# Moving key transposes under the first inversion and starting the second one a chunk early, with a slope that holds for any alpha

## The chip, the cores and the metric

The kernel runs on one core of one Trainium2 chip. The time is that of the device in microseconds from launch to end, the median of several runs. TensorE does the matrix products, VectorE and ScalarE take their results out of PSUM and do elementwise work, POOL (GpSimd) helps with elementwise work on SBUF, SP issues nearly all DMAs.

## What is computed

A delta-rule attention over 4 x 8 heads, 768 steps of 48 dimensions, and behind it a two-layer network with a parametric ReLU on the 3072 x 384 result:

```
k_n = k / (norm(k) + 1e-6)
for t in range(S):
    y[:, :, t] = q[t] @ state
    state += beta[t] * outer(k_n[t], v[t] - k_n[t] @ state)
x = y as (B*S, H*D)
h = x @ w_in                       # 384 -> 2048
g = max(h, 0) + alpha * min(h, 0)  # alpha per column, 0 to 0.3
out = g @ w_out                    # 2048 -> 384
```

## The kernel before, in words

The sequence is cut into 12 chunks of 64. A step is one chunk for two of the four batches, so there are 24 steps, n = 0 to 23, and two steps make a chunk of 256 tokens for the network. Within a chunk the recurrence becomes a triangular system, whose 32 x 32 blocks are inverted on VectorE for four steps at once (NJ = 4): inversion m serves steps 4m to 4m + 3.

All five queues are ordered by hand: instructions run on each engine in the order in which the program issues them. `weave` interleaves several generators in proportion to the parts that each has.

What a step needs before its recurrence:

- `load_early(n)` loads its keys into one of three buffers (SP). `squares(n)` squares them on ScalarE (L347) and adds up on VectorE (L349). `weigh(n)` takes the root (ScalarE, L357 and L358), a reciprocal (VectorE, L364) and two small products on POOL (L366, L367).
- `flips(n, q)` transposes the keys of step n and the queries of step q on TensorE (L377, four each); ScalarE copies them out (L398, L400).
- `grams(n)` multiplies keys with keys on TensorE (L424); VectorE weighs the result into `same` and `right` (L430, twice); `keep` copies parts with POOL or ScalarE (L473, L477).

An inversion, `eliminate(m)`, has 43 pieces: four transposes on VectorE (L489), a select on POOL (L506), 30 elimination steps of two VectorE instructions (L516, L522), eight transposes (L489). The first inversion is done by `eliminate_small` (L551 to L563) on half blocks, and `cross` puts the halves together (TensorE L593, L603, L610; ScalarE L598; VectorE L617, L619). `place` spreads the results (ScalarE L642, L648, L659; VectorE L638), `between_1` and `between_2` finish them (TensorE L709, L722, and L674 from step 4 on; VectorE L729).

The recurrence of a step is `through_state` (TensorE L763, VectorE L773 and L444), `solve` (L788, L792), `outputs` and `next_state` (L801, L817; VectorE L807, L825), `to_ffn` (transposes L840, copy L842).

The network reads `w_in` and `w_out` after a conversion: DMA into a staging place (L209), two ScalarE instructions (L225, L226, begun by `begin_in`) and two on VectorE (L235, L240, `convert`). `ffn_in(c)` makes 48 products for a chunk (L931), in eight pairs of columns that take turns in two PSUM banks `p_ffn`; behind each pair comes the activation: with `al_t` = alpha - 1, ScalarE makes relu((alpha - 1) h) for each of the two columns (L942) and VectorE adds h (L945). `ffn_out` makes the output products (L972 for chunks 0 and 1, L994 and L1245 later), `ffn_in_fast` serves chunks 8 to 11 with its own slope (L1197, L1202).

The order at the start: keys of steps 0 to 3 (`statics`), queries, then `busy(BUSY)`, which issues eight matrix products of 512 columns (L1389) whose results nobody reads, beside the first inversion on VectorE; `first_chunk` (steps 0 and 1); `second_pair` (steps 2 and 3), woven with `ffn_in(0)`, weight conversion, and the keys, norms and grams of steps 4 to 7; then a weave of `ffn_in(1)` with conversion, steps 8 and 9's keys and the first 15 pieces of the second inversion; then `ffn_out(0)` with the other 28 pieces; then `prelude(4)` with part of `ffn_out(1)`. Three PSUM pairs `p_pair` rotate as `big`.

## Time and profile before

| what | us |
|---|---|
| median of 3 runs | 668.64 (668.08 to 668.86) |
| the profiled execution | 667.61 |
| its span, first to last instruction | 665.9 |
| TensorE busy (share of the span) | 645.7 (97%) |
| VectorE busy | 468.3 (70%) |
| ScalarE busy | 287.9 (43%) |
| POOL busy | 97.8 (15%) |

A line of a timeline gives start, length, engine, line of the kernel, instruction, what it writes and reads, and in brackets how long its engine had been idle and what ended that. PE is TensorE, PEld its weight loads, DVE VectorE, ACT ScalarE. A matrix product of fp32 appears as two records. Records of neighbouring instructions on one engine overlap a little, so a start-to-start distance is shorter than a length.

### The profile page before, as it was taken

The page shows a single profiled execution, that of the slowest core. Times are in us where ns is not written, and L with a number is a line of the kernel's source. Part 1 is how long each engine was busy: PE and PEld are TensorE (multiplying, and loading weights), DVE is VectorE, ACT ScalarE, POOL GpSimd, SP SyncE. Part 2 cuts the span into 40 slices and gives each one's busy share as a digit, 9 for nine tenths or more (in the row PEclk, how much of TensorE's full clock was granted, in tenths as well). Part 3 has the DMA queues.
Part 4 walks back from the last instruction along what each step waited for, and adds up shares of the span by engine and source line. Part 5 has one row for each costly group of instructions (what it writes and reads, how often), then busy time and mean ns, then how long its engine had stood idle before and what let it go on. Part 6 is the DMA issues. An engine that isn't in the chain of part 4 may idle for free.

```text
span 665.9 us, 22115 instructions
## 1 busy us (share of the span) xinstructions
PE 645.7 (97%) x9551; PEld 570.0 (86%) x9551; DVE 468.3 (70%) x1084; ACT 287.9 (43%) x717; POOL 97.8 (15%) x201
## 2 busy tenths in 40 slices
PE   6989899999999999999999999999999999999997
PEld 5577788656688998988998998998999999999997
DVE  4965779868989958747949747858866656557363
ACT  4937767335456344334344334234236246052150
POOL 6000112001010000001000000000035044063260
PEclk9999999989999999999999999999999999999999
DMA  8847754211342032122111112112111210100000
GB/s 128 243 119 197 194 112 120 72 35 27 69 80 49 12 64 49 24 52 48 24 41 36 21 43 38 22 41 37 25 41 35 40 36 2 28 10 1 25 1 25
DMA packets 110962, 37.72 MB, mean 57 GB/s; under 512 B 104160, under 2 KB 107248, under 8 KB 110864
## 3 DMA queue, kind: packets, MB, share of 16 engines
q1 hardware_dynamic: 109088, 35.81, 24.6%
q8 instruction: 75, 1.23, 0.8%
q10 hardware_dynamic: 1776, 0.49, 0.4%
q14 instruction: 23, 0.19, 0.1%
HBM read 31.56 MB, written 4.72 MB: 54 GB/s over the span
## 4 chain that ended last, share of the span: by engine, by line
PE 84%; DVE 10%; ACT 3%; issue 2%; DMA 1%; ACTq 0%; DVEq 0%
PE p_ffn L931 22%; PE p_ffn L994 17%; PE p_more L1245 8%; PE p_more L1162 4%; PE p_ffn L1152 3%; PE p_ffn L1245 3%; PE p_pair L377 3%; PE p_ffn L1157 2%; PE p_pair L763 2%; PE p_pair L424 2%; PE p_pair L788 2%; PE p_pair L674 2%; PE p_pair L801 2%; DVE prod L516 2%; DVE block L522 2%; PE p_pair L1389 2%
## 5 line engine op out<-in xcount | busy, mean ns | idle before, releaser
L931 PE MATMUL p_ffn<-xt,w_in 128*128 128x256 f32 x768 | 175.0, 382 | 1.8 <-DVE act L945 1.0
L931 PEld LDWEIGHTS p_ffn<-xt,w_in 128*128 128x128 f32 x768 | 142.9, 190 | 21.9 <-DVE act L945 1.6
L942 ACT ACTIVATE act<-p_ffn,al_t 128x256 f32<-128x256 f32 x112 | 46.8, 468 | 75.5 <-PE p_ffn L931 75.2
L945 DVE TENSOR_TENSOR act<-act,p_ffn 128x512 f32<-128x512 f32 x56 | 38.2, 682 | 39.2 <-ACT act L942 39.0
L1186 POOL TENSOR_TENSOR k_t<-k_t 128x128 f32<-128x128 f32 (+1 forms) x48 | 32.2, 670 | 164.8 <-ACT k_t L1181 162.2
L522 DVE TENSOR_TENSOR block<-block,prod 128x30 f32<-128x30 f32 (+9 forms) x150 | 49.9, 333 | 5.2
L516 DVE TENSOR_TENSOR prod<-block 128x30 f32<-128x30 f32 (+9 forms) x150 | 48.9, 326 | 1.8
L842 ACT COPY xt<-p_pair 128x384 f32<-128x384 f32 x22 | 10.4, 480 | 91.1 <-PE p_pair L840 77.3
L994 PE MATMUL p_ffn<-w_out,act 128*128 128x192 f32 x288 | 49.7, 329 | 0.0
L366 POOL TENSOR_TENSOR beta_t<-beta_t,rec 128x8 f32<-128x8 f32 x24 | 6.3, 261 | 285.9 <-DVE rec L364 265.7
L994 PEld LDWEIGHTS p_ffn<-w_out,act 128*128 128x128 f32 x288 | 46.5, 190 | 0.6 <-DVE act L945 0.3
L1186 POOL TENSOR_TENSOR block<-block 128x128 f32<-128x128 f32 (+1 forms) x48 | 29.5, 616 | 14.7 <-ACT block L1181 12.1
L1152 PE MATMUL p_ffn<-xt,w_in 128*128 128x256 f32 x96 | 28.7, 380 | 0.0
L686 ACT COPY inv<-p_pair 32x256 f32<-32x256 f32 x40 | 14.4, 361 | 22.4 <-DVE u L792 21.4
L773 DVE TENSOR_TENSOR r<-v_raw,p_pair 64x192 f32<-64x192 f32 (+1 forms) x66 | 23.2, 352 | 1.2
L792 DVE TENSOR_TENSOR u<-p_pair,wgt 128x384 f32<-128x384 f32 x24 | 13.3, 556 | 15.1 <-PE p_pair L674 14.8
L1014 DVE TENSOR_TENSOR o_sb<-u,p_ffn 128x192 f32<-128x192 f32 x24 | 7.9, 351 | 20.2 <-PE p_ffn L994 19.8
L1245 PE MATMUL p_more<-w_out,act 128*128 128x192 f32 x128 | 22.0, 329 | 0.0
L349 DVE TENSOR_REDUCE norm<-ksq 128x8 f32<-128x384 f32 x24 | 13.1, 547 | 12.7 <-ACT ksq L347 12.6
L642 ACT ACTIVATE inv<-inverse,which 128x256 f32<-128x256 f32 x44 | 21.6, 504 | 0.2
L752 ACT COPY y<-p_pair 128x384 f32<-128x384 f32 x22 | 10.4, 478 | 26.0 <-PE p_pair L748 23.9
L1181 ACT COPY k_t<-p_more 128x512 f32<-128x512 f32 x16 | 9.4, 585 | 28.0 <-PE p_more L1162 25.1
(224 smaller groups left out, 1423.1 us busy)
## 6 DMA issues: line engine op xcount, KB each, us to landing
w_out<-in_moe_w_in_dram SPq DMA_DIRECT2D x12, 512.0 KB, 5.1
qp<-in_q_dram SPq DMA_DIRECT2D x48, 96.0 KB, 3.0
v_raw<-in_v_dram SPq DMA_DIRECT2D x48, 96.0 KB, 2.9
kl<-in_k_dram SPq DMA_DIRECT2D x96, 48.0 KB, 2.7
out_dram<-o_sb SPq DMA_DIRECT2D x92, 48.0 KB, 1.6
space_out<-in_moe_w_out_dram SPq DMA_DIRECT2D x11, 384.0 KB, 4.2
ke<-in_k_dram SPq DMA_DIRECT2D x43, 96.0 KB, 3.2
w_out<-in_moe_w_out_dram SPq DMA_DIRECT2D x5, 384.0 KB, 4.0
```

The costliest lines, as they stand in the source:

```text
L516: nc.vector.tensor_tensor(out=prod, in0=r[:, 0:j, j : j + 1].to_broadcast([128, j, n]), in1=r[:, j : j + 1, j + 1 : HB].to_broadcast([128, ...
L522: nc.vector.tensor_tensor(out=r[:, 0:j, j + 1 : HB], in0=r[:, 0:j, j + 1 : HB], in1=prod, op=ALU.add)
L642: nc.scalar.mul(out, x, which[:, i : i + 1])
L773: nc.vector.tensor_tensor(out=r[to, a], in0=v_in[to, a], in1=p[own, a, :, 0:D], op=ALU.subtract)
L931: nc.tensor.matmul(p_h[:, i], w_in[:, t, (f + i) * 128 : (f + i + 1) * 128], xt[:, t], start=(t == 0), stop=(t == KT - 1),)
L942: nc.scalar.activation(g[:, i], p_h[:, i], ACT.Relu, scale=al_t[:, f + i : f + i + 1])
L945: nc.vector.tensor_tensor(out=g, in0=g, in1=p_h, op=ALU.add)
L994: nc.tensor.matmul(p, x(i), w(i), start=(i == 0), stop=(i == FP - 1))
L1152: nc.tensor.matmul(p[:, f * 256 : f * 256 + 256], w(2, f), xt[:, 2], start=True, stop=False)
L1162: nc.tensor.matmul(q[:, j], a, b, start=True, stop=True)
L1186: nc.gpsimd.tensor_tensor(out=dst, in0=a, in1=b, op=ALU.add)
L1245: nc.tensor.matmul(p, x(i), w(i), start=(i == 0), stop=(i == FP - 1))
```

## The change

Three things are changed together.

1. The keys of steps 4, 5 and 6 are squared, transposed, and for 4 and 5 multiplied to grams, right behind the queries, between shorter fillers (`busy(2)` and three times `busy(1.25)` in place of `busy(8)`). One of the three PSUM pairs is set aside meanwhile to hold the two grams. Their norms, weights and gram evictions follow inside `first_chunk`. The fetch of the first six pieces of `w_in` is issued behind these keys' loads, and its conversions begin later: one ahead of the first inversion's end, three more behind the first cross products, two behind `between_2`. `second_pair` keeps only what is left of steps 6 and 7.
2. The second inversion, `eliminate(1)`, starts in `second_pair`: 4, 3, 3 and 3 of its pieces are woven in from the step behind `scale_v` on. Thirteen more, not fifteen, go beside `ffn_in(1)`, and the last 17 beside `ffn_out(0)`.
3. The activation becomes relu(-h) for both columns in one ScalarE instruction, and on VectorE, column by column, relu(-h) times (1 - alpha) plus h; so in `ffn_in` and in `ffn_in_fast`.

```diff
--- before.py
+++ after.py
@@ -307,7 +307,7 @@
     def slopes():
         p = ps_one()[:, 0:FT]
         nc.tensor.transpose(p, al_sb, ident[:FT, :FT])
-        nc.scalar.activation(al_t, p, ACT.Copy, bias=-1.0)
+        nc.scalar.activation(al_t, p, ACT.Copy, scale=-1.0, bias=1.0)
 
 
     beside = [const.tile([128, 2, G, D + C], FP32, name=f"beside{bp}") for bp in range(NB)]
@@ -340,14 +340,20 @@
         squares(n)
         now(weigh(n))
 
+    ksq = {}
+
+    def squared(n):
+        ksq[n] = work.tile([128, H, D], FP32, name="ksq", bufs=2)
+        nc.scalar.square(ksq[n], early(n)[:, :, 0:D])
+
+    def norms(n):
+        stats[n] = work.tile([128, H], FP32, name="norm", bufs=EARLY + 3)
+        nc.vector.tensor_reduce(out=stats[n], in_=ksq.pop(n), axis=AXX, op=ALU.add)
+
     def squares(n):
-        if n >= N:
-            return
-        ksq = work.tile([128, H, D], FP32, name="ksq", bufs=2)
-        nc.scalar.square(ksq, early(n)[:, :, 0:D])
-        norm = work.tile([128, H], FP32, name="norm", bufs=EARLY + 3)
-        nc.vector.tensor_reduce(out=norm, in_=ksq, axis=AXX, op=ALU.add)
-        stats[n] = norm
+        if n < N:
+            squared(n)
+            norms(n)
 
     def weigh(n):
         if n >= N:
@@ -424,9 +430,9 @@
             nc.tensor.matmul(
                 p[half(t), a, g], k_t[n][dims(a), g, half(t)], k_t[n][dims(a), g, half(t)]
             )
-        w = stats[n][1][:, 0:2, :, None].to_broadcast([128, 2, G, HB])
 
         def weighted(dst, cols):
+            w = stats[n][1][:, 0:2, :, None].to_broadcast([128, 2, G, HB])
             nc.vector.tensor_tensor(
                 out=dst.rearrange("p (a g) i -> p a g i", a=2), in0=p[:, :, :, cols], in1=w,
                 op=ALU.mult,
@@ -938,11 +944,12 @@
                         yield
 
             g = act_of(c, f // 2)
+            nc.scalar.activation(g, p_h, ACT.Relu, scale=-1.0)
             for i in range(2):
-                nc.scalar.activation(
-                    g[:, i], p_h[:, i], ACT.Relu, scale=al_t[:, f + i : f + i + 1]
+                nc.vector.scalar_tensor_tensor(
+                    out=g[:, i], in0=g[:, i], scalar=al_t[:, f + i : f + i + 1], in1=p_h[:, i],
+                    op0=ALU.mult, op1=ALU.add,
                 )
-            nc.vector.tensor_tensor(out=g, in0=g, in1=p_h, op=ALU.add)
             gs.append(g)
             if c >= FAST and f == FT // 2 - 2:
                 later = operand_sums(0)
@@ -1193,13 +1200,14 @@
                 )
 
             def below():
+                nc.scalar.activation(r, g, ACT.Relu, scale=-1.0)
+
+            def slope():
                 for f in range(2):
-                    nc.scalar.activation(
-                        r[:, f], g[:, f], ACT.Relu, scale=al_t[:, 2 * i + f : 2 * i + f + 1]
+                    nc.vector.scalar_tensor_tensor(
+                        out=g[:, f], in0=r[:, f], scalar=al_t[:, 2 * i + f : 2 * i + f + 1],
+                        in1=g[:, f], op0=ALU.mult, op1=ALU.add,
                     )
-
-            def slope():
-                nc.vector.tensor_tensor(out=g, in0=r, in1=g, op=ALU.add)
 
             due.put(PER * (i + 1) + {0: PER, FP - 1: 2}.get(i, 3), total)
             due.put(PER * (i + 2) + {FP - 2: 1, FP - 1: -4}.get(i, 2), below)
@@ -1424,22 +1432,30 @@
         next(middle)
         pause.append(ps_one())
         busy(1, pause[0])
-        begin_in(6)
+        begin_in(4)
         for i in both:
             scale_v(i)
             mask(i)
         convert(2)
+        for i in both:
+            norms(NJ + i)
         next(middle)
         busy(1.25)
         place(0, (0,))
+        rest = weigh(NJ) + weigh(NJ + 1)
         place(1, (0,), True)
         for i in both:
             place(i, (1,), True)
             now(between_1(i))
         busy(0.5, ps_ffn())
+        now(rest)
+        now(waiting)
+        big.append(aside)
         for i in both:
             place(i, (2,))
             now(between_2(i))
+        begin_in(6)
+        squared(NJ + 2)
         for i in both:
             now(through_state(i))
             now(solve(i))
@@ -1510,11 +1526,11 @@
         load_v(n)
     load_late(0)
     nc.sync.dma_start(out=al_sb, in_=moe_alpha.rearrange("(f p) -> f p", p=128))
-    fetch_in(n_in)
     squares(0)
     betas()
     for _ in statics(0, NJ - 1):
         pass
+    fetch_in(n_in)
     nc.scalar.copy(inside, ones)
     edges(0, edge)
     load_late(1)
@@ -1530,8 +1546,18 @@
     for i in range(2):
         place(i, (3,))
 
-    busy(BUSY)
-    begin_in(4)
+    aside = big.pop(0)
+    busy(2)
+    for n in range(NJ, NJ + 3):
+        if n < NJ + 2:
+            squared(n)
+        flips(n, N)
+        busy(1.25)
+        if n == NJ + 1:
+            waiting = grams(NJ, aside[:, :, 0 : G * C])
+    waiting += grams(NJ + 1, aside[:, :, 256 : 256 + G * C])
+    load_early(NJ + NKE)
+    begin_in(1)
     for _ in eliminate_small(0):
         pass
     n = 12
@@ -1552,60 +1578,52 @@
 
     def second_pair():
 
-        n = 2
-        both, x = (n, n + 1), NJ
+        n, last = 2, 2 * NJ - 1
+        both = (n, n + 1)
         halves = [cross(0, slice(i * H, i * H + H), edge, half_way) for i in both]
-        squares(x)
+        norms(last - 1)
+        now(weigh(last - 1))
         alongside(4, 2)
         for h in halves:
             next(h)
-        flips(x, n)
-        load_early(x + NKE)
+        flips(last, n)
+        load_early(last + 1)
         load_q(n + 2)
-        squares(x + 1)
+        squares(last)
         alongside(5, 2)
         next(halves[0])
-        flips(x + 1, n + 1)
-        load_early(x + 1 + NKE)
+        flips(N, n + 1)
+        load_early(last + 2)
         load_q(n + 3)
-        now(weigh(x))
+        now(weigh(last))
         place(n, (0,))
         alongside(4, 2)
         next(halves[1])
-        now(weigh(x + 1))
+        now(grams(last - 1))
         place(n + 1, (0,))
         alongside(4, 2)
         for i in both:
             now(between_1(i))
-        now(grams(x))
-        squares(x + 2)
+        now(grams(last))
+        load_early(last + 3)
         alongside(5, 3, (chain(*(placing(i, (1, 2, 3)) for i in both)), 6))
         for i in both:
             now(between_2(i))
-        now(grams(x + 1))
         for i in both:
             scale_v(i)
-        flips(x + 2, N)
-        load_early(x + 2 + NKE)
-        now(weigh(x + 2))
-        alongside(5, 3)
+        alongside(5, 3, (part(blocks, 4), 4))
         y = ps_big()
         pieces = []
         for i in range(2):
             pieces += through_state(n + i, None, y[:, :, i * G * D : (i + 1) * G * D])
         now(pieces)
-        squares(x + 3)
-        alongside(5, 3)
+        alongside(5, 3, (part(blocks, 3), 3))
         y = ps_big()
         pieces = []
         for i in range(2):
             pieces += solve(n + i, y[:, :, i * G * D : (i + 1) * G * D])
         now(pieces)
-        now(grams(x + 2))
-        flips(x + 3, N)
-        load_early(x + 3 + NKE)
-        now(weigh(x + 3))
-        alongside(5, 2)
+        alongside(5, 2, (part(blocks, 3), 3))
         pieces = []
         for i in both:
             y = ps_big()
@@ -1614,15 +1632,14 @@
         for i in both:
             load_late(i + 2)
             load_v(i + 3)
-        alongside(5, 2)
+        alongside(5, 2, (part(blocks, 3), 3))
         for i in both:
             to_ffn(i)
-        now(grams(x + 3))
         alongside(IN_PARTS - 42, 1)
 
+    blocks, SOON, LAST = eliminate(1), 13, 6
     second_pair()
     fetch_out(len(stages))
-    blocks, SOON, LAST = eliminate(1), 15, 6
     weave(
         (part(conv_out, PARTS_OUT - 10 - LAST), PARTS_OUT - 10 - LAST), (ffn_in(1), IN_PARTS - 4),
         (statics(2 * NJ, FIRST + 3), 2 * (FIRST + 4 - 2 * NJ) + 1), (part(blocks, SOON), SOON),
@@ -1633,7 +1650,7 @@
     load_early(FIRST + NJ + NKE)
     load_q(NJ + 2)
     weave(
-        (conv_out, OUT_PARTS // 2), (part(blocks, WHOLE + PIECES - SOON), WHOLE + PIECES - SOON),
+        (conv_out, OUT_PARTS // 2), (part(blocks, WHOLE + PIECES - 13 - SOON), WHOLE + PIECES - 13 - SOON),
         (ffn_out(0, True), OUT_PARTS),
     )
```

## The prediction

> **What bounds the kernel now.** First the page's busy line, then the table of stretches, whose columns are busy time and instruction count of each engine, granted clock, DMA share and GB/s.
>
> ```profile
> PE 645.7 (97%) x9551; PEld 570.0 (86%) x9551; DVE 468.3 (70%) x1084; ACT 287.9 (43%) x717; POOL 97.8 (15%) x201
> ```
> ```profile
> 20.00:30.00 10.00, 10.00 (x108) 4.48 (x102) 9.01 (x31) 9.61 (x20) 0.00 (x0) 1.00 0.96 239
> ...
> 48.70:72.30 23.60, 20.38 (x508) 16.98 (x508) 13.24 (x31) 17.18 (x41) 2.19 (x6) 1.00 0.79 188
> 72.30:95.20 22.90, 22.77 (x521) 19.96 (x522) 18.15 (x42) 14.59 (x37) 4.51 (x10) 1.00 0.62 168
> 95.20:119.30 24.10, 23.92 (x176) 20.33 (x175) 21.63 (x57) 17.60 (x42) 4.71 (x10) 1.00 0.45 113
> 119.30:140.10 20.80, 20.80 (x66) 11.96 (x64) 17.75 (x51) 4.68 (x11) 0.78 (x2) 1.00 0.16 39
> 140.10:150.00 9.90, 8.40 (x143) 5.32 (x142) 4.55 (x11) 5.35 (x14) 0.41 (x2) 0.83 0.26 61
> 150.00:222.00 72.00, 69.43 (x1254) 54.38 (x1247) 65.08 (x156) 36.13 (x97) 6.24 (x14) 1.00 0.27 52
> 222.00:500.00 278.00, 278.00 (x4115) 256.79 (x4114) 201.10 (x478) 105.07 (x275) 12.01 (x27) 1.00 0.19 37
> ```
>
> From 222 us on TensorE never rests, so what happens earlier only shifts the end, microsecond for microsecond. Before that VectorE is nearly as full as TensorE: 18.2 of 22.9 us in the stretch of the second pair of steps, 21.6 of 24.1 in the second chunk's input products, 65.1 of 72 after 150. Between 119 and 140 TensorE (output products of the first chunk) is the longer of the two. Next the timelines of TensorE and VectorE around the edits:
>
> ```profile
> 20.17 9.22 PE L1389 MATMUL p_pair<-k_t,ident 112*128 112x512 f32 x16
> ...
> 119.32 20.81 PE L972 MATMUL p_ffn<-w_out,act 128*128 128x384 f32 x64
> 141.63 0.69 PE L674 MATMUL p_pair<-diag,right 32*32 32x32 f32 x32 [1.50 <-ACT diag L648]
> ```
> ```profile
> 78.40 1.11 DVE L773 TENSOR_TENSOR r<-v_raw,p_pair 128x192 f32<-128x192 f32 x3
> ...
> 91.33 0.69 DVE L945 TENSOR_TENSOR act<-act,p_ffn 128x512 f32<-128x512 f32 x1 [1.35 <-ACT act L942]
> ...
> 95.39 0.69 DVE L945 TENSOR_TENSOR act<-act,p_ffn 128x512 f32<-128x512 f32 x1 [2.25 <-ACT act L942]
> ...
> 139.19 1.94 DVE L489 STREAM_TRANSPOSE turned<-block 128x256 f32<-128x256 f32 x4
> ```
>
> The 9.22 us of L1389 are filler beside the first inversion. At 140 TensorE waits 1.50 us: the second inversion's transposes end on VectorE at 141.1, ScalarE copies, L674 starts. Idle time of VectorE between 72 and 120 that later work could fill is small: 1.35 and 2.25 above, and 0.50, 0.94, 0.44 in the same timeline, 5.5 in all.
>
> [...] the clock reads 0.63, 0.50 and 0.74 in the three 1.5 us slices from 143.5 to 148, right after the wait at 140. [...] the rows L430 and L945 show 415 to 419 and 682. [...] L398 (immediate, 512 wide) takes 583, L942 (pointer, 256) 468, two of them 0.84 us: so one 512-wide instruction in their place saves some 0.25.
>
> **The change, part by part.** Sums are against the profiled execution: span 665.9, own time 667.61, 1.03 below the median of 668.64. I add the sum to the median.
>
> *Filler replaced (20 to 30 us).* Filler falls from 8 units to 2 + 3 x 1.25 = 5.75; three key transposes (L377) and two gram groups (L424) come in. The 16 filler records start 0.85 us apart until 24.5 and 0.43 after, so at this clock: 4 records 3.6, first transpose 0.9, three fillers at 1.08 = 3.2, two transposes at 0.48, two gram groups at 0.55. Sum 9.8 against 9.2: the cross products (L593) start **0.6 later**. Nothing hides that: VectorE's transposes, which L593 needs, are ready at 28.05, and all after it is one chain. Bounds: -0.5 (warm earlier) to +2 (a transpose waits for a copy behind ScalarE's zeros, which end at 23.7).
>
> *Queues.* SP issues steps 4 to 6's keys (six DMAs, 3.9 us at 0.65 each) ahead of the six w_in pieces. w_in then lands near 22 to 29; its first conversion is now at about 29 and four more follow the first cross product, so ScalarE does not wait. The loads behind (late keys, v, q) are not read before 46. Step 7's key DMAs come after its buffer is free at 24.5. Cost 0. If DMA is still full, cost up to 1. On ScalarE squares, copies and weighing (some 4 us) fit its idle 1.2 before 38.1 and 4.0 before 44.2 once conversions are spread. On VectorE two norms (1.0) fit before L617 (idle 1.15), and two reciprocals and four gram evictions (1.7) fit the idle 3.19 before L729; POOL's eight small operations and four copies run while it is idle from 19 to 60. Cost 0; uncovered, up to 1.
>
> *48.7 to 72.3.* Here the same transposes and grams remain as before (step 6's and 7's grams move up where 4's stood). ScalarE loses a square (0.43) and that 0.25 per slope, ahead of the 0.89 wait of L722 for it: **-0.6**. TensorE's waits on "issue" (0.27, 0.59, 1.21) move to other places with the changed instruction stream: -1 to +1, taken as -0.4. With the first part: -0.4 at 72.
>
> *72 to 120.* TensorE loses three transposes and grams here, 2.8 us. VectorE is what counts. Removed: three gram evictions (0.73 each), a norm 0.46, two reciprocals 0.24: 2.9. Added: 26 pieces of the second inversion instead of 15, the difference being elimination steps 11 to 21, which the timeline has from 122.5 to 133.3 with 1.95 of conversions between: 8.9. The slope, thirteen pairs of columns from here: one 512-wide L945 (0.60 start to start) becomes two 256-wide instructions with a per-partition scalar. No row shows that form. Below, two plain ones: 2 x 0.34, +0.08. Above: L638, 256 wide with such a scalar at double rate, takes 0.349 where L235's 0.42 for 512 at the same rate implies 0.29, so the scalar costs 0.06, twice: +0.20. A gain is excluded, since two fixed costs replace one. I take **+0.18**, 2.3 in all. Net 2.9 out, 11.2 in: +8.3. Of the idle 5.5 the 0.94 hangs on a ScalarE queue that waits for w_out DMAs, themselves released by VectorE's conversions; 4.5 to 5 can be filled. So the last slope of the second chunk ends **3.4 later**. Order of the waits: four turns ahead of r delay L773 and so L788; elimination steps ahead of u delay L801; those ahead of y delay L840; then L945 holds one of two p_ffn banks and L931 waits. L972's second product needs the last L945, hence with -0.4, **+3.0** at 120.
>
> *120 to 150.* VectorE now has 9 steps (5.6), 8 transposes (4.1) and 3 of other work beside 20.8 of TensorE: done by 138. L648 still stands behind two o_sb copies, the second ending at 140.64, so only **0.55** of the 1.50 goes; the copies are late next. [...] half rate for 3.4 us cost **1.7**, which I count as saved. +0.75 here.
>
> *After.* 150 to 222: eight slopes at 0.18 on a VectorE with 65.1 of 72 us, half of it reaching TensorE: **+0.7**. After 222: VectorE at 72% absorbs it, ScalarE is 0.25 shorter per pair: 0, bounds -0.5 to +1.5.
>
> Sum: -0.4 + 3.4 - 0.55 - 1.7 + 0.7 = +1.45, with rounding upward for the unfilled waits **+1.6**: 670.2, slower by just over the 0.2% (1.3 us) that a measurement of this kernel can tell from no change.
>
> **Rivals.** *Wash.* The scalar costs nothing (+0.08 per pair: 1.0 and 0.3 in place of 2.3 and 0.7): -0.1, giving 668.5. For it: L945's PSUM operand costs nothing extra either. Against: L638. *Faster: VectorE fits.* Place: the second chunk's slopes. If also the "issue" wait before 67.5 vanishes (-1.2) and all idle is filled (-1.0), the debt at 120 falls to +0.4 with the cheap slope, the wait and throttle give back 2.2: 666.5. It decides where the last L945-like slope ends before 120.5. For it: TensorE does lose 2.8 us of work there. Against: VectorE was already full from 73.7 to 90. *Worse.* The throttle still falls (+1.7), or falls in the new waits of 80 to 97; 672 to 673.6.
>
> **Numbers.** Full VectorE, clock kept or not: 0.50 (own range 668.8 to 673.6). Wash 0.25, faster 0.25. Range 666.0 to 673.6: it leaves out the faster case's far end and a throttle with a late start. Chances: faster 0.26, same 0.26, slower 0.48.
>
> **What would show it.** Right: VectorE without idle from 74 to 122; the two new slope instructions 0.47 to 0.49 each; new TensorE waits before L788, L801 and L931 between 80 and 97 on VectorE; L972 of the first chunk starting near 122; the wait before L674 near 1.0; clock 1.00 around 145. Wrong: L972 starting at or before 119.3, or VectorE idle over 3 us between 74 and 122.

## The result, and the profile after

The changed kernel takes 675.89 us (median of 4 runs, 674.84 to 676.93) against 668.47 for the kernel before: a ratio of 1.0116, interval 1.0081 to 1.0151. It is slower, as forecast to be likeliest, but by 7.4 us, not 1.6, and above the range. Here and below, medians are over all runs of a kernel, while ratios and their intervals leave out the few runs that lie more than 1.5% above the fastest of the same kernel, which makes a ratio a little kinder to a kernel that scatters much. The profiled execution took 674.84 us, its span 673.1 (before: 667.61 and 665.9).

The page of the kernel after, its busy line and the clock in 40 slices of the span:

```profile
PE 651.7 (97%) x9551; PEld 574.8 (85%) x9551; DVE 490.9 (73%) x1180; ACT 264.7 (39%) x621; POOL 92.6 (14%) x201
...
PEclk9958999999999999999999999999999999999999
```

The same row of the kernel before:

```profile
PEclk9999999989999999999999999999999999999999
```

VectorE does 22.6 us more and ScalarE 23.2 less: the slope's work has moved. The news is in the third and fourth slice: the clock falls at some 34 us, long before any place where the prediction had looked for a fall. The table of stretches of the kernel after (same columns as before; the stretches answer to those shown there) bounds it:

```profile
20.00:30.05 10.05, 9.78 (x100) 5.63 (x92) 9.10 (x31) 7.92 (x19) 0.00 (x0) 1.00 1.03 337
30.32:33.73 3.41, 2.63 (x152) 1.74 (x140) 3.38 (x10) 2.18 (x5) 0.00 (x0) 1.00 0.50 74
33.73:54.21 20.48, 20.18 (x414) 16.06 (x417) 8.64 (x23) 7.47 (x19) 2.35 (x8) 0.50 0.23 53
57.50:81.20 23.70, 22.03 (x573) 18.82 (x574) 15.45 (x39) 16.36 (x37) 3.36 (x8) 1.00 0.74 184
81.20:103.60 22.40, 20.64 (x386) 17.08 (x385) 21.41 (x59) 12.35 (x25) 1.43 (x2) 1.00 0.67 177
103.60:127.20 23.60, 23.35 (x171) 19.36 (x170) 23.10 (x63) 14.14 (x30) 3.23 (x8) 1.00 0.38 106
127.20:148.50 21.30, 21.03 (x66) 11.94 (x64) 12.57 (x37) 4.70 (x11) 0.74 (x2) 1.00 0.17 38
148.50:158.00 9.50, 7.74 (x149) 5.09 (x149) 2.21 (x6) 5.25 (x14) 0.40 (x2) 1.00 0.28 64
158.00:230.00 72.00, 68.84 (x1244) 53.97 (x1243) 65.99 (x164) 34.40 (x90) 6.25 (x14) 1.00 0.27 52
```

From 33.73 to 54.21, six windows of 3.41 us (the edges of the clock are whole multiples of that apart, as shown further down), TensorE runs at exactly half rate and is nominally busy throughout (20.18 of 20.48). That is nearly all of the first chunk from the cross products on. The timeline of TensorE in the kernel after shows the moment, and then products whose records are nearly twice as long as they were:

```profile
30.09 1.26 PE L599 MATMUL p_pair<-turned,sums 32*32 32x16 f32 x128
31.28 1.12 PE L1397 MATMUL p_pair<-k_t,ident 112*128 112x512 f32 x2
32.34 0.61 PE L609 MATMUL p_pair<-act,inverse 32*32 32x16 f32 x26
34.02 0.34 PE L609 MATMUL p_pair<-act,inverse 32*32 32x16 f32 x6 [1.08 <-issue]
...
41.83 3.63 PE L715 MATMUL p_pair<-diag,right 64*64 64x32 f32 x64
...
57.53 1.99 PE L937 MATMUL p_ffn<-xt,w_in 128*128 128x256 f32 x8 [0.62 <-ACT xt L848]
...
127.25 0.81 PE L979 MATMUL p_ffn<-w_out,act 128*128 128x384 f32 x2
128.33 20.23 PE L979 MATMUL p_ffn<-w_out,act 128*128 128x384 f32 x62 [0.27 <-DVE more L949]
149.44 0.69 PE L680 MATMUL p_pair<-diag,right 32*32 32x32 f32 x32 [0.87 <-ACT diag L654]
```

(Line numbers after are 4 to 8 higher: L593, L603 and L610 are now L599, L609 and L616; L709 is L715, L722 L728, L931 L937, L945 L949, L972 L979, L674 L680.) TensorE ran out of instructions for 1.08 us in the middle of a cross product; at the end of that window the clock was cut. L715 took 3.63. The kernel before, with its own wait for instructions in L801:

```profile
29.33 1.40 PE L593 MATMUL p_pair<-turned,sums 32*32 32x16 f32 x128
...
36.95 2.06 PE L709 MATMUL p_pair<-diag,right 64*64 64x32 f32 x64 [0.22 <-ACT diag L642]
...
45.94 0.32 PE L801 MATMUL p_pair<-u,a_t 64*64 64x48 f32 x6 [0.86 <-issue]
...
48.66 0.70 PE L931 MATMUL p_ffn<-xt,w_in 128*128 128x256 f32 x2 [0.62 <-ACT xt L842]
```

Milestones on TensorE, each the start of the first instruction named, from the timelines:

| us | before | after |
|---|---|---|
| cross products of steps 0 and 1 (L593, L599) | 29.33 | 30.09 |
| input products of chunk 0 (L931, L937) | 48.66 | 57.53 |
| output products of chunk 0 (L972, L979) | 119.32 | 127.25 |
| finishing of step 4 (L674, L680) | 141.63 | 149.44 |
| end of the span | 665.9 | 673.1 |

The kernel is 8.87 behind at the first input products, and gains 1.7 back afterwards. Of the 8.87, 0.76 is there at the cross products; the other 8.11 lie between there and the input products. The stretch between these two, after and then before:

```profile
30.09:57.53 27.44, 25.75 (x669) 20.33 (x662) 14.95 (x37) 11.75 (x27) 2.35 (x8) 0.63 0.34 79
```
```profile
29.33:48.66 19.33, 17.48 (x664) 13.88 (x663) 13.24 (x31) 7.27 (x16) 0.00 (x0) 1.00 0.44 111
```

The same products (some 665 records) keep TensorE busy for 25.75 us in place of 17.48, 8.27 more, and it is idle for 1.69 in place of 1.85. So **half rate is all of these 8.11**, 1.4 us for each of six windows. The wait of 1.08 costs nothing by itself: the kernel before has 0.86 on "issue" in L801 and 0.22 ahead of L709, which are gone.

### The profile page after: what moved, and what is told of

It is laid out like the page before. It is cut to its first block, busy times and chain, and to the rows that moved or that the text cites. A ratio compares the mean times of both kernels' runs of the same rounds, so it can differ in the third digit from the quotient of the medians.

```text
span 673.1 us, 22128 instructions
## 1 busy us (share of the span) xinstructions
PE 651.7 (97%) x9551; PEld 574.8 (85%) x9551; DVE 490.9 (73%) x1180; ACT 264.7 (39%) x621; POOL 92.6 (14%) x201
## 3 DMA queue, kind: packets, MB, share of 16 engines
q8 instruction: 75, 1.23, 0.8%
## 4 chain that ended last, share of the span: by engine, by line
PE 82%; DVE 12%; ACT 4%; issue 2%; DMA 1%; ACTq 0%; DVEq 0%
PE p_ffn L937 19%; PE p_ffn L1001 17%; PE p_more L1253 8%; PE p_more L1169 4%; PE p_ffn L979 4%; PE p_ffn L1159 3%; PE p_ffn L1253 3%; PE p_ffn L1164 2%; PE p_pair L383 2%; PE p_pair L807 2%; PE p_pair L680 2%; PE p_pair L794 2%; PE p_pair L430 2%; PE p_pair L769 2%; DVE block L528 2%
## 5 line engine op out<-in xcount | busy, mean ns | idle before, releaser
L937 PE MATMUL p_ffn<-xt,w_in 128*128 128x256 f32 x768 | 176.0, 383 | 2.8 <-DVE act L949 1.6
L937 PEld LDWEIGHTS p_ffn<-xt,w_in 128*128 128x128 f32 x768 | 142.4, 190 | 24.4 <-issue 2.7
L949 DVE SCALAR_TENSOR_TENSOR act<-act,al_t,p_ffn 128x256 f32<-128x256 f32 x112 | 48.5, 475 | 27.0 <-ACT act L947 26.8
L947 ACT ACTIVATE act<-p_ffn 128x512 f32<-128x512 f32 x56 | 33.3, 595 | 84.7 <-PE p_ffn L937 84.6
L1193 POOL TENSOR_TENSOR k_t<-k_t 128x128 f32<-128x128 f32 (+1 forms) x48 | 29.6, 616 | 166.7 <-ACT k_t L1188 164.1
L1193 POOL TENSOR_TENSOR block<-block 128x128 f32<-128x128 f32 (+1 forms) x48 | 27.9, 582 | 16.6 <-ACT block L1188 14.1
L779 DVE TENSOR_TENSOR r<-v_raw,p_pair 64x192 f32<-64x192 f32 (+1 forms) x66 | 23.2, 352 | 1.1
L1207 DVE SCALAR_TENSOR_TENSOR act<-block,al_t,act 128x256 f32<-128x256 f32 x32 | 19.1, 637 | 5.1 <-ACT block L1203 5.1
L648 ACT ACTIVATE inv<-inverse,which 128x256 f32<-128x256 f32 x44 | 21.6, 504 | 0.3
L436 DVE TENSOR_TENSOR same<-p_pair,wgt 128x256 f32<-128x256 f32 x24 | 10.0, 419 | 15.6 <-PE p_pair L430 13.0
```

Source lines behind the costliest of these rows:

```text
L779: nc.vector.tensor_tensor(out=r[to, a], in0=v_in[to, a], in1=p[own, a, :, 0:D], op=ALU.subtract)
L937: nc.tensor.matmul(p_h[:, i], w_in[:, t, (f + i) * 128 : (f + i + 1) * 128], xt[:, t], start=(t == 0), stop=(t == KT - 1),)
L947: nc.scalar.activation(g, p_h, ACT.Relu, scale=-1.0)
L949: nc.vector.scalar_tensor_tensor(out=g[:, i], in0=g[:, i], scalar=al_t[:, f + i : f + i + 1], in1=p_h[:, i], op0=ALU.mult, op1=ALU.add,)
L1193: nc.gpsimd.tensor_tensor(out=dst, in0=a, in1=b, op=ALU.add)
```

## The experiments

In what follows the time of one kernel scatters from run to run with the number of half-rate windows in it. Each run lists its mean clock c; windows = (1 - c) x 2 x span / 3.41. The 55 runs of the kernel before in one comparison have 0 to 11 of them, and a straight line through them gives 666.2 us at none and 0.25 us more per us at half rate, some 0.9 per window (0.9 to 1.3 within six of the kernels below). The profiled span of the changed kernel also ends at half rate, from 672.02 to 673.12, and this counts with the rest; in the kernel before that fall comes at 666.12, just behind the span's end (665.90). The changed kernel has 6 or 7 in every run. So I give the median, the ratio with its interval, and how many runs have at most two windows.

Theory A, the one at the start: part 1 puts some 150 instructions ahead of the cross products, TensorE's queue runs empty in a bad place (a wait on "issue"), and the clock falls and stays low for the first chunk. Its rivals: theory B, the thinner filler lets the clock fall, not the wait; theory C, VectorE's debt (the work that the early second inversion or the dearer slope adds to it) is the cost and the clock an accident. Theory D, that a window must hold a certain amount of array work, came from the first traces.

**The slope alone.**

```diff
-nc.scalar.activation(g[:, i], p_h[:, i], ACT.Relu, scale=al_t[...])   # for each column
-nc.vector.tensor_tensor(out=g, in0=g, in1=p_h, op=ALU.add)
+nc.scalar.activation(g, p_h, ACT.Relu, scale=-1.0)
+nc.vector.scalar_tensor_tensor(out=g[:, i], in0=g[:, i], scalar=al_t[...], in1=p_h[:, i], ...)
```

> The kernel before with the new slope alone. Theories A and B: the slope is no part of the loss, 667.5 to 669.5 with the clock as before. Theory C: VectorE between 150 and 222 us hands its 8 x 0.18 on, 669.5 to 671.

Measured: 671.02 (20 runs), ratio 0.9994, interval 0.9964 to 1.0025; 9 of 20 with at most two windows, about as the kernel before. The median lies above what A and B expected, but the kernel before took 669.99 beside it, and the ratio leaves no room for a loss of 1.2%. The slope is not the cause.

**The second inversion late.** The changed kernel with part 2 undone (the pieces out of `second_pair`, 15 in the next weave).

> The changed kernel with the second inversion started where it was before (none of it in second_pair, 15 pieces beside ffn_in(1), 28 beside ffn_out(0)). Theories A and B: half clock in the first chunk stays, and the early start of the inversion is worth something, so 676 to 678.5 with the wait of 1.5 us at the end of ffn_out(0) back. Theory C: VectorE's debt in the second pair is gone, 671 to 673.

Measured: 673.88 (20 runs), ratio 1.0062, interval 1.0042 to 1.0082; 6 to 8 windows in all 20. The median lies between the two forecasts. Part 2 is not the cause of the half rate, which stays with part 1; but it has a share in the loss, since without it the ratio is lower by 0.0054, some 3.6 us, with intervals that barely touch. The profiled span is 672.1 against 673.1, both with six windows in the first chunk. Between the input and output products of chunk 0 it takes 67.90 us against 69.72 with the early start and 70.66 in the kernel before.

**The gram groups moved.** Part 1's grams of steps 4 and 5 go from the filler to behind `between_1`.

```diff
         busy(1.25)
-        if n == NJ + 1:
-            waiting = grams(NJ, aside[...])
-    waiting += grams(NJ + 1, aside[...])
...
+        waiting.extend(grams(NJ, aside[...]))
+        waiting.extend(grams(NJ + 1, aside[...]))
         busy(0.5, ps_ffn())
```

> The changed kernel with the two gram groups of steps 4 and 5 issued behind between_1 instead of ahead of the first cross products; filler and transposes stay. 128 TensorE instructions go from ahead of the cross products to behind them, so the wait on issue at 32.8 us should go elsewhere. Theory A (the half clock from 33.7 to 54.2 us is the loss, and the 1.1 us wait in the window before it brought it on): clock stays full, 667 to 668.5. Theory B (half clock too, but for the thin filler, wait or not): half clock from about 34 stays, 675 to 677. Theory C (VectorE's debt is the loss): 675 to 677 at whatever clock.

Measured: 674.03 (667.97 to 676.88, 12 runs), ratio 1.0049, interval 1.0018 to 1.0081. Two of the 12 runs have no window at half rate (667.97 and 669.57), ten have four to seven. One and the same kernel thus takes some 6 us more when the clock falls, whatever VectorE has to do: against theory C. But the full clock that A expected came in two runs only. The profiled run is one of these two. Its timeline:

```profile
28.78 1.42 PE L599 MATMUL p_pair<-turned,sums 32*32 32x16 f32 x128
...
38.25 1.41 PE L715 MATMUL p_pair<-diag,right 64*64 64x32 f32 x42 [0.86 <-issue]
...
50.39 1.78 PE L937 MATMUL p_ffn<-xt,w_in 128*128 128x256 f32 x7 [0.62 <-ACT xt L848]
```

With the clock held, cross products to input products take 21.61 us, two gram groups more included, where the changed kernel takes 27.44. The queue runs empty here too, later, and the clock stays. In the other ten runs it fell; there is no trace of those.

**More filler ahead of the cross products.** `busy(1.25)` between the transposes becomes `busy(2)`.

> The changed kernel with the three fillers of 1.25 units at 2 units each: 2 + 3 x 2 = 8, as before, and the same number of instructions. Cross products start 1.9 us later. Theory A (the issue wait brought the half clock on): wait and half clock stay, about 677. Theory B (thin filler): clock full, 668 to 670. Theory C (VectorE's debt): 676 to 678 at whatever clock.

Measured: 678.7 (4 runs), ratio 1.0116, interval 1.006 to 1.0173, six windows in each. The wait in L609 is 1.25 and half rate begins at 38.06. Filler ahead of the cross products does not help: against theory B.

**The wait made in the kernel before.** 38 tiny products are put behind `slopes()`, as many instructions (152) as the change adds ahead of the cross products; and as a control 64 (256 instructions, about as many as one transfer of instructions carries by the estimate of 255 further down).

```diff
+    for _ in range(38):            # 64 in the control
+        nc.tensor.matmul(...)      # 32 x 32 by 16, nobody reads it
```

> The kernel before with 38 products of 32 x 32 x 16 (152 TensorE instructions, their results not read) put into TensorE's wait for alpha at 14 us. The instructions of the first cross products then stand at the same count as in the changed kernel, with the whole filler of 8 units. Theory A (a wait for the next block of instructions inside the small cross products brings the half clock on, and which instruction it falls on is set by their count): a wait of about 1 us inside L603, half clock for some six windows of 3.4 us in every run, 673 to 676. Theory B (the thinner filler of the change): no change from before, 667 to 671.

> Control: the kernel before with 64 such products, 256 instructions, so that the blocks fall on the same instructions as without them. Theories A and B: as before, 667 to 671; the products themselves fit the wait for alpha.

Measured: 676.85 (4 runs, seven or eight windows in each), ratio 1.0103, interval 1.0052 to 1.0155. The profile has the wait (in L610) and half rate from 35.90 to 56.38:

```profile
30.92 1.12 PE L1389 MATMUL p_pair<-k_t,ident 112*128 112x512 f32 x2
32.89 0.62 PE L603 MATMUL p_pair<-act,inverse 32*32 32x16 f32 x28 [0.84 <-ACT act L598]
...
35.77 1.32 PE L610 MATMUL p_pair<-inverse,act 32*32 32x16 f32 x88
38.56 0.73 PE L610 MATMUL p_pair<-inverse,act 32*32 32x16 f32 x40 [1.47 <-issue]
```

The control, with more padding, takes 672.93 (20 runs, none to eight windows), ratio 1.0068, interval 1.004 to 1.0096, above the 667 to 671 expected. But it is no clean control in time: its tiny products take 7.00 us and did not fit the wait, and its cross products start at 32.11 in place of 29.33; with 152 instructions they start at 29.56. By windows it is one: 9 of 20 runs have at most two, about as the kernel before (20 of 51). So 152 instructions of no use, without any of the change, bring the kernel before to the changed kernel's time, all but 0.2 us of it by the clock, and 256 leave the clock much as it was. That speaks for the position in the instruction stream; but in this profile the window that falls, 32.48 to 35.90, has its idle time, some 0.6, from the end of a wait for ScalarE and from 0.23 on "issue"; the long wait on "issue" came after it. The wait on "issue" is one way into the trap, not the only one.

**The same padding in the changed kernel.** 32 tiny products, to shift the wait away.

> The changed kernel with 32 such products (128 instructions), which brings the cross products close to where they stood against the blocks before. Filler and grams stay as changed. Theory A: no wait inside L609, first-chunk clock full in most runs, 667 to 670. Theory B: half clock as in the changed kernel, 675 to 677.

Measured: 675.98 (20 runs), ratio 1.008, interval 1.0051 to 1.0109. The expectation of no wait was wrong: 2.78 us of it, in L599. The tiny instructions moved the wait and made it longer; the runs have one to nine windows.

**A longer pause.** `busy(1, pause[0])` ahead of the second cross product becomes 2.

> The changed kernel with the filler behind the first cross products (while ScalarE copies them) at 2 units in place of 1: 0.86 us more of dense work in the window that fell to half rate, and 0.86 us more for the next block to arrive. Theory A: the wait inside L609 shrinks from 1.1 to 0.3, so the added filler costs nothing, clock full, 667 to 669. Theory B with the filler ahead of the cross products as the cause: half clock stays, 676.

Measured: 675.31 (16 runs), ratio 1.0094, interval 1.0073 to 1.0114. The wait in L609 is gone and one of 1.01 stands in L616; half rate from 38.32 to 51.98. Better by one or two windows, and no cure.

**What a window must hold.** By now ten traces were at hand, and I worked out, from the records of the products, how full each window of 3.41 us was: each record counts for its columns at the full-rate pace (a filler record of 512 columns starts 0.43 us after the one before it, in proportion for fewer), times the share of 128 x 128, the largest tile in any record and taken here for the whole array, that its rows and columns take. By this weight, an assumption that is tested below, a 32 x 32 product counts a sixteenth. The kernel after's window 30.32 to 33.73 comes to 0.85 us of 3.41, though PE is "busy" 2.63; the kernel before's four windows from 27.83 to 41.48 come to 1.74, 1.18, 1.25 and 1.03. Three kernels with filler added inside the first chunk and one with denser filler tested it:

```diff
-waits, pause = iter([0.5] * 2), []
+waits, pause = iter([0.75] * 2), []
-busy(1, pause[0])
+busy(1.5, pause[0])
-busy(1.25)
+busy(1.5)
-busy(0.5, ps_ffn())      # three places
+busy(1, ps_ffn())        # 1, 1 and 0.75
```

> The changed kernel with more filler in the first chunk: the pause 1.5 units instead of 1, the waits between cross products 0.75 instead of 0.5, then 1.5 instead of 1.25, and the three of 0.5 become 1, 1 and 0.75 (about 2.1 us of filler more, the computation unchanged). Theory D (a window of 3.41 us in which the products fill the array to less than about a quarter, by area and time, falls to half rate, and the thin stretches of the first chunk then keep it there): the clock is full in the first chunk in most runs and the time is 667.5 to 671 although filler was added. Rival A (the wait on 'issue' alone starts it): half clock as before the edit, 676 to 678. Rival C (VectorE's debt is the cost): 676 to 678, with the clock's windows irrelevant to the time.

Measured: 676.03 (20 runs), ratio 1.0064, interval 1.0032 to 1.0097; but of two kinds, eight runs with none or one window at 669.2 to 670.4, twelve with five to nine at 675.8 to 681.1. The profiled one is of the first kind, with a wait of 0.75 on "issue" in L609 and of 1.13 in L616 and a full clock there. So the wait alone does not decide; the forecast "in most runs" was a miss.

> The kernel before with the same added filler in the first chunk. Theory D: fewer windows at half clock there than the kernel before has, 667 to 669 with narrower scatter: the filler's 2 us are paid back. Otherwise: the filler's own cost on top of the time before, 670 to 672.

Measured: 672.04 (20 runs), ratio 1.0025, interval 0.9994 to 1.0055; seven of 20 with at most two windows. A miss: the filler is not paid back here. The profile, of a run with six windows, shows one way: the wait now falls into L709, and the window 37.00 to 40.41, with a nominal 2.60 us busy, holds only 0.64 of full-array work and falls.

```profile
33.59:37.00 3.41, 3.41 (x143) 2.30 (x138) 1.65 (x4) 0.14 (x1) 0.00 (x0) 1.00 0.77 138
37.00:40.41 3.41, 2.60 (x66) 2.09 (x65) 1.06 (x4) 0.73 (x2) 0.00 (x0) 1.00 0.39 141
40.41:54.07 13.66, 13.66 (x265) 10.24 (x263) 4.98 (x10) 2.13 (x5) 0.00 (x0) 0.50 0.22 74
```

> The changed kernel with its filler products made of 128 rows and 128 columns in place of 112 rows (the same count of instructions and of moving columns, so the same time, and some 14% more of the array at work). Theory D with its threshold near 0.9 us of full-array work in a window: the window around the wait goes from 0.85 to about 0.95, the half clock in the first chunk goes away in many runs, 667 to 672. If the rows don't count, or the wait on 'issue' alone decides: 675 to 677, half clock as it was.

Measured: 677.15 (4 runs, six or seven windows), ratio 1.0099, interval 1.0066 to 1.0131. A miss for the edit. In this profile the window with the wait (1.16) runs from 33.52 to 36.93; with the fuller filler it comes to 0.90, and it fell. Since windows of about 0.9 do both (see the count below), this doesn't tell whether the rows count. Where a window begins differs from trace to trace: the first edge behind 30 us is at 30.11 here, 30.32 in the changed kernel, 31.24 in the kernel before.

> The changed kernel with the gram groups of steps 4 and 5 moved behind the between products, the early start of the second inversion undone, and the same added filler in the first chunk. Theory D: clock full in the first chunk, 666 to 669, no slower than the kernel before. Otherwise: half clock stays in most runs, 673 to 676.

Measured: **667.77** (20 runs), ratio 0.9977, interval 0.9952 to 1.0001; 16 of 20 with at most two windows, as expected of a held clock. This is the changed kernel with the grams moved, the filler added and part 2 undone.

**Which of the three it was.** Three more kernels take that apart: with the early second inversion kept, without the added filler, and with the old slope.

> The changed kernel with only the gram groups of steps 4 and 5 moved behind the between products and the added filler of 2.1 us; the second inversion starts early as in the change. If the two edits together keep the clock (groups out of the thin place, filler to hold the array up) and the early start costs the 1 to 2 us that it cost elsewhere: at most two windows at half rate in most runs, median 668.5 to 670. If the early start mattered for the clock too: 672 to 676.

> The changed kernel with the gram groups moved and the early start undone, without the added filler. If the filler is needed: half clock in the first chunk in most runs as with the moved groups alone, 672 to 674. If the moved groups were enough and the early start was the disturbance: 666 to 668.

> The kernel before with the first part of the change alone (keys of steps 5 to 7 beside the first inversion), the gram groups moved and the filler added; the slope and the second inversion as before. If the slope is worth nothing, as it was alone: within 0.15% of the version with the new slope, 666.8 to 668.8. If ScalarE's shorter work is what pays, or VectorE's longer work costs, once the clock holds: over 1 us away from it, either way.

Measured: early inversion kept, 668.66 (12 runs), ratio 0.9989, interval 0.996 to 1.0018, ten of 12 with at most two windows, as the first of its two expectations has it. Without the filler, 670.53 (20 runs), ratio 1.0022, interval 0.9997 to 1.0048, four of 20 (neither of the two expectations: between them). Old slope, **667.09** (20 runs), ratio 0.9967, interval 0.9946 to 0.9988, 16 of 20, and none over four, within the 0.15% of a slope that is worth nothing. (Its expectation counts the keys from one: they are those of steps 4 to 6.)

So filler and moved grams hold the clock together, and neither alone does; with the late inversion, 2 us of filler that computes nothing take the ratio from 1.0022 to 0.9977 and the runs with at most two windows from four of 20 to 16, with the early one from 1.0049 to 0.9989 and from two of 12 to ten. The early start of the second inversion leaves the clock alone (ten of 12 runs, 16 of 20 without it) and costs 0.9 us of median (668.66, 667.77), the new slope 0.7 (667.77, 667.09); the intervals of the two ratios overlap widely in both cases, so here neither is established. Part 1 with these two is faster than the kernel before by 0.3%, the only one of 15 versions whose interval excludes no gain, and it does so narrowly. Its TensorE goes through the first chunk like this:

```profile
29.16 1.26 PE L599 MATMUL p_pair<-turned,sums 32*32 32x16 f32 x128
30.34 1.56 PE L1395 MATMUL p_pair<-k_t,ident 112*128 112x512 f32 x4
31.83 0.68 PE L609 MATMUL p_pair<-act,inverse 32*32 32x16 f32 x32
32.44 0.91 PE L1395 MATMUL p_pair<-k_t,ident 112*128 112x384 f32 x2
33.28 0.68 PE L609 MATMUL p_pair<-act,inverse 32*32 32x16 f32 x32
...
37.91 0.65 PE L715 MATMUL p_pair<-diag,right 64*64 64x32 f32 x16 [0.28 <-ACT diag L648]
38.85 1.52 PE L715 MATMUL p_pair<-diag,right 64*64 64x32 f32 x45 [0.29 <-issue]
```

The waits are down to 0.28 and 0.29, dense products (L1395) stand between all small ones, and the stretch's clock reads full:

```profile
30.05:46.00 15.95, 15.19 (x505) 11.18 (x494) 10.24 (x28) 9.65 (x22) 2.36 (x8) 1.00 0.48 90
```

**The count over all 17 traces**, over windows that end before 200 us, with a record's work laid from its start on: of 804 windows that began at full rate, 27 were followed by half rate. All 19 that held up to 0.88 us of full-array work were; of 20 between 0.88 and 1.13, eight; of 765 above, none. Seven of the eight had TensorE idle for over 1 us, and so had two of the twelve that stayed up. Laid evenly over the records, the work gives bounds that differ by less than 0.1.

Ranking by busy time does not separate them: 2.63 us busy fell (after, 0.85), and 2.55 stayed up (grams moved, 37.31 to 40.72, 0.95). Its best bound leaves 23 of the 804 on the wrong side, the bound on array work seven. On the way back, of 36 half-rate windows below 0.95 none was followed by full rate, of 15 above 1.25 all were; between them both occur.

This is a fit to these traces, not a direct trial: no run changed a window's fill and nothing else. Nor does it settle the weight. On the way down, weighing by rows alone or by columns alone leaves six on the wrong side, no weight at all nine; on the way back, of 71 windows, the array's share leaves three, rows or columns alone seven and six, no weight 19. So small products count for less than their busy time, but that a 32 x 32 product counts just a sixteenth is not shown.

## Why the prediction was wrong, step by step

**The step that failed is *Filler replaced*.** Its +0.6 for the start of the cross products was right (0.76). But it was worked out "at this clock", and "all after it is one chain" was taken to mean that the 0.6 is simply handed on: what stands behind it, up to 48.7, got no entry. I counted durations of what was moved and did not count instructions, nor what share of the array they fill. The throttle was treated as a matter of waits, at 140 and, in the rival *Worse*, from 80 to 97; the tiny products between 29 and 48 with filler wedged in between were not read as a place with a margin. Missing there: the 8.1 of half rate. That the direction was forecast right is luck: it was to come from VectorE between 72 and 120, where in the event the kernel gained.

- *Queues*, 0: nothing contradicts it; no TensorE wait in the first chunk names a DMA or a conversion.
- *48.7 to 72.3* and *72 to 120*: forecast -0.6 - 0.4 to 72, then +3.4. From the input products to the output products it came out at **-0.94** (70.66 to 69.72). The 2.8 us that TensorE loses are real: with the late inversion the stretch is 2.76 shorter, 2.49 of it busy time of TensorE (67.14 to 64.65). The second inversion's debt is real but smaller: +1.82 there. The mis-sized term is "TensorE loses three transposes and grams here, 2.8 us. VectorE is what counts": the 2.8 were put at nothing and came through nearly in full. VectorE is as full as foreseen (45.99 of 47.50 us from 80.70 to 128.20), but it had more room than the 5.5 read from the timeline, of which 4.5 to 5 were to be filled: the prediction's own table leaves it 7.2 from 72.30 to 119.30, and 1.5 are left in the two stretches that answer to it (81.20 to 127.20). In them its busy time grew by 4.7 (39.78 to 44.51), where +8.3 was forecast; which term of the 8.3 was too large stays open. With the late inversion, the stretch that answers to 81 to 104 leaves it 5.3 us:

```profile
81.90:104.30 22.40, 21.13 (x393) 18.29 (x393) 17.10 (x40) 12.77 (x27) 0.00 (x0) 1.00 0.61 164
```

  The early start fills 4.3 of these (21.41 busy after) and leaves TensorE 1.8 us idle in place of 1.3. Two of the waits named are there, small: 0.36 before L807 (was L801), 0.20 and 0.23 before L937; before L794 (was L788) there is none.
- *Slope, +0.18 per pair*: L949 takes 475 ns, a pair 0.86 to 0.88 from start to end against 0.69 (forecast: each 0.47 to 0.49). The forecast's "double rate" for L638 was an estimate, for which the rows show only that L235 takes 414 ns for 512 columns where L945 takes 682; L949's 475 against the 415 to 419 of L430 puts the scalar at 0.06 here too. The group in the kernel after:

```profile
L949 DVE SCALAR_TENSOR_TENSOR act<-act,al_t,p_ffn 128x256 f32<-128x256 f32 x112 | 48.5, 475 | 27.0 <-ACT act L947 26.8
L947 ACT ACTIVATE act<-p_ffn 128x512 f32<-128x512 f32 x56 | 33.3, 595 | 84.7 <-PE p_ffn L937 84.6
```

 In all it costs nothing that shows alone (0.9994); the 0.7 of median with the clock held are not established.
- *120 to 150*: the wait before L680 fell from 1.50 to 0.87, forecast 0.55 less, and behind ScalarE as said. The clock stayed at 1.00 there, as the forecast had guessed: no window from 139.54 to 153.20 held less than 2.05 us of full-array work by the count above, where in the kernel before that from 140.47 to 143.88 held 1.11 and was followed by half rate. But this half window was worth 0.73, not 1.7, which was an estimate (half of its 3.41): from L674 to the next one 6.29 us in the kernel before, 5.56 after. Much of what the full clock saves turns into a wait of 0.89 for ScalarE (L648) before the next L680.
- *After*: from step 4's finishing to the end 524.3 before and 523.7 after, with the 0.73 of the half window in it; +0.7 was expected beside that. The slope's cost to 222 was some 0.6, measured against the same stretch without a half window (73.97 less 0.73 before, 73.82 after); and 0.45 came back after 222, where 0 was taken.
- *Rivals*: *Worse* had the right mechanism, a fall of the clock, at the wrong place and with one window in place of six; *Faster* fell, yet its premise, that part 1 takes work away which VectorE can make up for, holds once the clock does.
- The range left out what lies behind the cross products altogether; the bound of +2 on this step was one of a wait alone.

The edges of the clock are whole multiples of 3.41 us apart in the traces: 24.41, 143.88, 147.29 and 666.12 in the kernel before, 23.49, 33.73, 54.21 and 672.02 in the kernel after (the first of each is where its clock record begins). A window need not be idle to be followed by half rate: the one here had TensorE busy for 2.63 of 3.41 us.

How the instructions come, the page shows in one line, the same before and after (q8 is a DMA queue that carries instructions):

```profile
q8 instruction: 75, 1.23, 0.8%
```

75 transfers of 1.23 MB in all are 16.4 KB each, and TensorE's 2 x 9551 records over 75 are 255: if the queue serves TensorE alone, one transfer brings some 255 of its instructions, which is an estimate. The 128 records of L599, with as many weight loads, are 256 in 1.26 us: about a whole transfer.

That a wait on "issue" is a wait for the next transfer fits the padding runs, in which 152 instructions without use moved it, and the DMA records of the 17 traces bear it out. From 20 to 250 us they have 58 such waits of over 0.2 us on TensorE, and every one ends 1.20 to 1.83 us after a q8 transfer has ended and 2.2 to 3.1 after it began; of moments drawn at random 8% do the former. In the kernel after the transfer runs from 31.32 to 32.66, and the wait in L609 ends at 34.02. How many instructions TensorE holds ahead, the runs do not show.

## What to carry over

Where TensorE works in small tiles, its busy share says little about its clock (here a window busy for 2.63 us was followed by half rate, one busy for 2.55 was not; by the count they held 0.85 and 0.95): count small products for less, as here by the part of the array that they fill, window by window, and leave a margin, since the windows began elsewhere in each trace. Before filler is replaced by useful work, ask what the filler was holding up: useful transposes and grams in place of such products cost 8 us in the first chunk here. With the grams moved, 2 us more of products that nobody reads were worth 3 to 4; in the kernel before, the same filler was not paid back. And when a change moves hundreds of tiny instructions, count instructions as well as time; a short wait for the next ones did no harm in some windows and stood in a thin one at the start of six at half rate.

## What the runs showed of the hardware that I had not expected

- A window of 3.41 us at full rate was followed by half rate in all 19 cases in which its products held up to 0.88 us of full-array work by the count above; here it held 0.85, although TensorE counted as busy for 2.63 us of it. Half rate then lasted six windows: five held 0.64 to 0.71, the sixth 1.13, and full rate followed.
- One half-rate window cost 0.9 us on the average over the runs of the kernel before, 1.4 in the first chunk, 0.73 at step 4's finishing, where much of the gain turned into a wait for ScalarE.
- TensorE waited 0.2 to 2.8 us for instructions, at places that move with the number of instructions ahead of them, and went on 1.2 to 1.8 us after a transfer of 16.4 KB of instructions had ended.
- VectorE's `scalar_tensor_tensor` of 256 fp32 with a per-partition scalar took 475 ns in L949, some 60 more than `tensor_tensor` of that width in L430 (415 to 419); in L1207, which reads no PSUM, it took 637 and 700.
